# W2 moved into the B stage as eight 64x64 events, with weight rows on two DMA queues

## The chip, the cores and the metric

The kernel runs on one core of one Trainium2 chip. The metric is the device time of one execution in microseconds. All runs quoted are of the state called fast unless the text says otherwise. Engines: PE is TensorE, PEld its weight loads, DVE is VectorE, ACT is ScalarE, POOL is GpSimd, SP is SyncE, which here only issues DMAs.

## The reference, cut to what matters

Two attention blocks read the same `x` (2048 x 1024) and a gate mixes their outputs. Both have 32 heads of 32.

```python
# A: linear attention
q, k, v = split(x @ A_wqkv)
pq, pk = phi(q), phi(k)                    # phi(t) = (t+1 if t > 0 else exp(t)) + 1e-6
kv  = einsum("bhsd,bhse->bhde", pk, v)     # one 32x32 matrix per head
o   = einsum(pq, kv) / (einsum(pq, z) + 1e-6)
a   = o @ A_wo
# B: sliding window of 8 keys, dilation 2, softmax; b = (...) @ B_wo
return g * a + (1 - g) * b
```

Since `o @ A_wo` is linear in `kv`, the kernel folds the 32 small `kv` matrices into `A_wo` once. `z` is the sum of `pk` over `s`. The folded matrix is called W2, and it overwrites the tile `WoA`. Nothing reads W2 before the output stage, the last one.

## The kernel before: the parts that matter

The stages follow each other on TensorE: keys of A (`pk_ps`), G = xᵀ·phi(k) (`g_ps`), the small `kv` matrices (`kv_ps`), values of B mixed with the W2 events (the V stage), values of B and queries of A in turn (the query stage), the B stage (keys, queries, scores, outputs of the window attention, in 64x64 mode), and the output stage.

The first loads. TensorE needs `x` transposed and the key weights in order of `kt`, the 128-row slice of the contraction:

```python
load_wk(nc.scalar, 0)          # weight row kt on ScalarE's queue
load_xT(0, 1, 0, 4)            # a DMA transpose, on SyncE's queue
load_wk(nc.sync, 1)
load_xT(1, 1, 0, 4)
for kt in range(2, KT):        # KT = 8
    load_wk(nc.sync, kt)
    if kt % 2 == 0:
        load_xT(kt, 2, 0, 4)
```

W2 in the V stage, as four events of sixteen matmuls, each on its own 32x32 part of the array:

```python
def w2_event(g, half):
    w2p = [ps_1.tile([P, 512], F32, ...) for _ in range(4)]        # four PSUM tiles
    for j in range(4):
        for r in range(4):
            rs = slice(32 * r, 32 * r + 32)
            nc.tensor.matmul(w2p[r][32 * j:32 * j + 32, :],
                             lhsT=KVT[rs, 4 * g + j, (r % 2) * 32:(r % 2) * 32 + 32],
                             rhs=WoA[half][rs, 4 * g + j, :], start=True, stop=True)
    for r in range(4):
        (nc.scalar.copy if r % 2 else nc.vector.tensor_copy)(out=WoA[half][:, 4 * g + r, :], in_=w2p[r][:])
```

The B stage works in units: one unit is four 64x64 matmuls that run side by side. There are 64 units to a head block and eight head blocks. Other work is hung in between at a unit number. The score batches share one PSUM buffer (`ps_s`, one buffer of two banks):

```python
p_ = 64 * c + (43, 55, 75, 86, 97)[m // 4]           # cut: the last block differs a little
events.append((p_, lambda g=g: scores(g)))            # takes the tile with tag "s" of ps_s
events.append((p_ + 14, lambda g=g: pv(g)))
```

At the end of the query stage VectorE still has the last block of A's queries to finish (phi, then `normalize`: two passes of 1024 elements, some small ones, and the product with the reciprocal). That work needs the last matmuls of the query stage.

The softmax here doesn't subtract the row's maximum and nothing guards it: scores larger than these inputs give would overflow.

Of the kernel before, what the change touches and what calls it, by code (L numbers as in the profile page):

```python
# [9 lines left out]
ALU = mybir.AluOpType  # L10
BF16 = mybir.dt.bfloat16
F32 = mybir.dt.float32
# [3 lines left out]
P = 128  # L16
# [23 lines left out]
def kernel(  # L40
# [11 lines left out]
    nc = tc.nc  # L52
# [3 lines left out]
    x = A_x[0].rearrange("(m two) d -> two m d", two=2)  # L56
# [5 lines left out]
    H = 32  # L62
    Dh = D // H
    KT = D // P
# [29 lines left out]
    def load_xT(kt, n, t0, t1):  # L94
        nc.sync.dma_start_transpose(out=xT[:, kt:kt + n, t0 * P:t1 * P],  # L95
                                    in_=rows(x, t0 * P, t1 * P)[:, kt * P:(kt + n) * P])

    def load_wk(eng, kt):
        eng.dma_start(out=WkA[:, kt, :], in_=A_wqkv[kt * P:(kt + 1) * P, D:2 * D])  # L99

    ones = nc.const_aps.tensor(1.0, [P, P], BF16)
    with tc.manual_schedule(engines={SP, mybir.EngineType.Activation}):
        load_wk(nc.scalar, 0)
        load_xT(0, 1, 0, 4)
        load_wk(nc.sync, 1)
        load_xT(1, 1, 0, 4)
        for kt in range(2, KT):
            load_wk(nc.sync, kt)
            if kt % 2 == 0:
                load_xT(kt, 2, 0, 4)  # L110
        for t in range(4, NB):
            nc.sync.dma_start_transpose(out=xT[:, :, t * P:(t + 1) * P], in_=rows(x, t * P, (t + 1) * P))  # L112
        for t in range(0, NB, 4):
            load_rows(nc.sync, t, t + 4)
        gw_row = consts.tile([P, D], BF16, name="gw_row")
        nc.sync.dma_start(out=gw_row[:], in_=gate_w.partition_broadcast(P))  # L116
        WvA = load_w("WvA", A_wqkv, 2 * D, "wb")
        WoA = load_w("WoA", A_wo, 0, "wo")
        WvB = load_w("WvB", B_wqkv, 2 * D, "wc")
# [18 lines left out]
    for slot in range(2):  # L138
        nc.gpsimd.memset(qsel[:, slot:slot + 1], 0.0)
        for pair in range(2):  # L140
            r = 64 * pair + 32 * slot
# [3 lines left out]
    omg = consts.tile([P, NB], F32, name="omg")  # L145
    zrow = consts.tile([P, D], F32, name="zrow")
    KVT = consts.tile([P, KT, 64], BF16, name="KVT")

    small3 = ctx.enter_context(tc.tile_pool(name="small3", bufs=2))

    def phi(work, dst, pj):
        e = work.tile([P, 512], F32, name="e", tag="e")
# [4 lines left out]
    with tc.manual_schedule(engines={PE}):  # L157

        with ExitStack() as s1:
# [39 lines left out]


            side = []
            for t in range(1, NB):
                side.append(lambda t=t: nc.vector.tensor_tensor(
                    out=zacc[:], in0=zacc[:] if t > 1 else pk[:, 0, :], in1=pk[:, t, :], op=ALU.add))
            side.append(lambda: nc.gpsimd.partition_all_reduce(zrow[:], zacc[:], P, bass_isa.ReduceOp.add))
            for t in range(NB):
                side.append(lambda t=t: nc.vector.tensor_tensor_reduce(
# [24 lines left out]
            for g in range(2):  # L232
                kvp = ps_pj.tile([P, 512], F32, name="kv_ps", tag="pj")[:, 0:256].rearrange("p (c d) -> p c d", c=4)
                for c in range(4):
                    for kt in range(KT):
                        for j in range(2):
                            cols = slice(c * P + 64 * j, c * P + 64 * j + 64)
                            nc.tensor.matmul(kvp[64 * j:64 * j + 64, c, :], lhsT=WvA[g][:, kt, cols],
                                             rhs=G[g][:, kt, cols], start=(kt == 0), stop=(kt == KT - 1))
                nc.vector.tensor_copy(out=KVT[:, 4 * g:4 * g + 4, :], in_=kvp)  # L240
            WkB = load_w("WkB", B_wqkv, D, "wb")


# [28 lines left out]



            def w2_event(g, half):
                def go():
                    w2p = [ps_1.tile([P, 512], F32, name="w2_ps", tag="p1") for _ in range(4)]
                    for j in range(4):
                        for r in range(4):
                            rs = slice(32 * r, 32 * r + 32)  # L280
                            nc.tensor.matmul(w2p[r][32 * j:32 * j + 32, :],
                                             lhsT=KVT[rs, 4 * g + j, (r % 2) * 32:(r % 2) * 32 + 32],
                                             rhs=WoA[half][rs, 4 * g + j, :], start=True, stop=True)
                    for r in range(4):
                        (nc.scalar.copy if r % 2 else nc.vector.tensor_copy)(
                            out=WoA[half][:, 4 * g + r, :], in_=w2p[r][:])
                return go

            def v_units(t):
                def mm(half, kt, st):  # L290
                    if kt == 0:
                        st["pj"] = bank1()
                    nc.tensor.matmul(st["pj"][:], lhsT=xT[:, kt, t * P:(t + 1) * P], rhs=WvB[half][:, kt, :],  # L293
                                     start=(kt == 0), stop=(kt == KT - 1))
                    if kt < KT - 1:
                        return
                    v = Vst[t % 2]
                    nc.scalar.copy(out=v[:, half * 16:(half + 1) * 16, 0:Dh],  # L298
                                   in_=st["pj"][:].rearrange("p (h e) -> p h e", h=16))
                    if half == 1:  # L300
                        nc.sync.dma_start(out=vd[t * P:(t + 1) * P, :], in_=v.rearrange("p h e -> p (h e)"))
                        if t % 8 == 7:
                            load_v(t // 8)
                for half in range(2):
                    st = {}
                    for kt in range(KT):
                        yield lambda half=half, kt=kt, st=st: mm(half, kt, st)

            def normalize(t, pq, pn, prod):
                nc.vector.tensor_tensor(out=prod, in0=pq, in1=zrow[:], op=ALU.mult)  # L310
                den = small3.tile([P, H], F32, name="den", tag="den")
                nc.vector.tensor_reduce(out=den[:], in_=prod.rearrange("p (h e) -> p h e", h=H),
                                        axis=mybir.AxisListType.X, op=ALU.add)
                nc.vector.tensor_scalar(out=den[:], in0=den[:], scalar1=1e-6, scalar2=None, op0=ALU.add)
                nc.vector.reciprocal(out=den[:], in_=den[:])

                nc.vector.tensor_scalar(out=den[:], in0=den[:], scalar1=ratio[:, t:t + 1], scalar2=None, op0=ALU.mult)
                for g in range(2):
                    nc.vector.tensor_tensor(
                        out=pn[:, 512 * g:512 * g + 512].rearrange("p (r j e) -> p j r e", r=4, j=4),  # L320
                        in0=pq[:, 512 * g:512 * g + 512].rearrange("p (j r e) -> p j r e", r=4, j=4),
                        in1=den[:, 16 * g:16 * g + 16].rearrange("p (j r o) -> p j r o", r=4, o=1)
                        .broadcast_to([P, 4, 4, Dh]), op=ALU.mult)

            def qa_units(t, bank, evacuate):
                def mm(half, kt, st):
                    if kt == 0:
                        st["pj"] = bank()
                    nc.tensor.matmul(st["pj"][:], lhsT=xT[:, kt, t * P:(t + 1) * P], rhs=WqA[:, kt, half * 512:half * 512 + 512],  # L329
                                     start=(kt == 0), stop=(kt == KT - 1))  # L330
                    if kt == KT - 1:
                        evacuate(t, half, st["pj"])
                for half in range(2):
                    st = {}
                    for kt in range(KT):
                        yield lambda half=half, kt=kt, st=st: mm(half, kt, st)
# [5 lines left out]
                    normalize(t, pq, pn, prods[t % 2])  # L342
                    nc.sync.dma_start(out=pqd[t * P:(t + 1) * P, :], in_=pn)

            units = [u for t in range(4) for u in v_units(t)]
            w2_event(0, 0)()
            interleave(units, [(20, w2_event(0, 1)), (32, w2_event(1, 0)), (44, w2_event(1, 1))])
            for t in range(12):
                for u in v_units(4 + t):
                    u()  # L350
# [9 lines left out]
        with ExitStack() as s2:  # L360
# [139 lines left out]
            for g, (c, m, n) in enumerate(BATCHES):  # L500
                p_ = 64 * c + ((43, 55, 75, 86, 97) if c < KT - 1 else (43, 55, 75, 83, 92))[m // 4]
                events.append((p_, lambda g=g: scores(g)))
                events.append((p_ + (14 if c < KT - 1 or m < 8 else 12), lambda g=g: pv(g)))

            def between(a, b):
                return [(p_ - a, f) for p_, f in events if a <= p_ < b]

# [31 lines left out]
            def qa_output(t, half):  # L539
                def lhsT(r, kt, j):  # L540
                    return xT[64 * r:64 * r + 64, kt, t * P + 64 * j:t * P + 64 * j + 64]

                def rhs(r, kt):
                    return WqA[64 * r:64 * r + 64, kt, half * 512:half * 512 + 512]

                def evacuate(ps, part):
                    if part == 0:
                        nc.scalar.copy(out=raw[:, t - 12, half * 512:(half + 1) * 512], in_=ps[:])
                return lhsT, rhs, evacuate
# [93 lines left out]
```

## Time and profile before

| | before |
|---|---|
| median of 5 runs | 474.04 us |
| profiled span | 472.34 us |
| TensorE busy | 466.3 us (99%) |
| start to first `g_ps` matmul | 61.44 us |
| last `kv_ps` to first query matmul (V stage and W2) | 19.18 us |
| query stage | 79.52 us |
| B start to first scores | 9.62 us |

TensorE is busy nearly all the time, so a change counts only where TensorE issues less or waits less. The busy table of the page of before gives engine, busy us, share, instructions:

```profile
PE 466.3 (99%) x5735; PEld 244.8 (52%) x5765; DVE 277.3 (59%) x601; ACT 169.1 (36%) x272; POOL 15.3 (3%) x30
```

The timeline of TensorE around one W2 event of before: start, length, engine, line, operation, out<-in, shape, count.

```profile
122.55 1.24 PE L293 MATMUL p_ps<-WvB,xT 128*128 128x512 bf16 x5
123.72 0.43 PE L281 MATMUL w_ps<-WoA,KVT 32*32 32x512 bf16 x16
124.09 2.76 PE L293 MATMUL p_ps<-WvB,xT 128*128 128x512 bf16 x12
126.78 0.43 PE L281 MATMUL w_ps<-WoA,KVT 32*32 32x512 bf16 x16
```

The lengths overlap (a 128x512 matmul is 0.38 us long, 0.216 us after the one before), so one reads starts. The last V matmul before the event starts at 123.41 us, the first after it at 124.09, where 0.216 us is the rule between 128x512 matmuls. The event costs 0.47 us.

The timeline of TensorE at the start, of before; brackets give idle time and what ended it:

```profile
4.74 4.14 PE L167 MATMUL pk_ps<-WkA,xT 128*128 128x512 bf16 x15
9.19 0.39 PE L167 MATMUL pk_ps<-WkA,xT 128*128 128x512 bf16 x1 [0.31 <-DMA xT<-in_A_x_dram]
9.86 2.32 PE L167 MATMUL pk_ps<-WkA,xT 128*128 128x512 bf16 x10 [0.28 <-DMA WkA<-in_A_wqkv_dram]
```

Two waits: the third transpose and weight row 3. From start to start they cost 0.47 and 0.45 us.

VectorE's timeline at the B start (217.51 us) of before:

```profile
218.25 0.43 DVE L154 TENSOR_SCALAR e<-e 128x512 f32<-128x512 f32 x1
218.71 0.69 DVE L155 SCALAR_TENSOR_TENSOR tmp<-p_ps,e 128x512 bf16<-128x512 f32 x1
219.43 1.22 DVE L310 TENSOR_TENSOR tmp<-tmp,zrow 128x1024 f32<-128x1024 bf16 x1
220.69 1.22 DVE L312 TENSOR_REDUCE den<-tmp 128x32 f32<-128x1024 f32 x1
...
222.55 0.24 DVE L317 TENSOR_SCALAR den<-den,ratio 128x32 f32<-128x32 f32 x1
222.83 1.29 DVE L319 TENSOR_TENSOR tmp<-tmp,den 128x512 bf16<-128x512 bf16 x2
```

There is no hole in it: for 6.6 us of the B stage VectorE has nothing to spare.

### The profile page before, as it was taken

Reading aid. Unit: us, or ns where it says so; the run is one execution under the profiler, and the core shown is the slowest. Engines: PE = TensorE matmul, PEld = TensorE weight load, DVE = VectorE, ACT = ScalarE, POOL = GpSimd, SP = SyncE. Lnnn points to the kernel's source line nnn. Section 1 sums busy time; section 2 is a strip of 40 time slices with the busy share of each in tenths; the row PEclk is TensorE's granted clock in tenths of the full one; section 3 lists DMA queues with packets and bytes.
Section 4 is the critical chain, followed back from the end, with each engine's and each line's share of the span. In section 5 each row is a group of like instructions: output and inputs, shape, how many; then the busy total and the mean of one; then the engine's idle time right before and its main releaser. Section 6 shows DMA issues by size and latency. Waiting matters only on the chain.

```text
span 472.3 us, 13141 instructions
## 1 busy us (share of the span) xinstructions
PE 466.3 (99%) x5735; PEld 244.8 (52%) x5765; DVE 277.3 (59%) x601; ACT 169.1 (36%) x272; POOL 15.3 (3%) x30
## 2 busy tenths in 40 slices
PE   8999999999999999999999999999999999999997
PEld 5444444444444444445666666666664444444444
DVE  0496689990329999999567676767560049800000
ACT  1343321102533333333555555555551134221122
POOL 3300000500000000000000000000000000000000
PEclk9999999999999999999999999999999999999999
DMA  9999970000644233527326526432463843221101
GB/s 199 196 240 377 348 266 0 0 1 0 207 135 108 98 138 132 154 97 243 108 57 104 105 55 95 101 82 63 93 164 67 187 113 78 70 54 45 35 33 46
DMA packets 96716, 55.40 MB, mean 117 GB/s; under 512 B 70162, under 2 KB 86546, under 8 KB 96658
## 3 DMA queue, kind: packets, MB, share of 16 engines
q1 hardware_dynamic: 91618, 50.10, 41.4%
q10 hardware_dynamic: 5040, 4.46, 3.0%
q8 instruction: 45, 0.74, 0.7%
q14 instruction: 13, 0.11, 0.1%
HBM read 26.10 MB, written 15.86 MB: 89 GB/s over the span
## 4 chain that ended last, share of the span: by engine, by line
PE 86%; SPq 11%; DMA 2%; issue 1%; ACT 0%
PE q_ps L387 27%; PE d_ps L584 12%; PE p_ps L293 12%; PE e_ps L584 11%; PE g_ps L218 11%; PE p_ps L329 9%; SPq L112 4%; SPq L82 4%; DMA WvB<-in_B_wqkv_dram 2%; PE po L466 2%; PE s2b L444 2%; SPq L95 1%; SPq L99 1%; SPq L116 1%; SPq L90 0%
## 5 line engine op out<-in xcount | busy, mean ns | idle before, releaser
L387 PE MATMUL q_ps<-xT,WqB 64*64 64x512 bf16 x1024 | 68.3, 377 | 0.0
L387 PE MATMUL q_ps<-xT,WkB 64*64 64x512 bf16 x1024 | 67.9, 377 | 0.0
L154 DVE TENSOR_SCALAR e<-e 128x512 f32<-128x512 f32 x64 | 27.0, 422 | 64.5 <-ACT e L153 64.5
L293 PE MATMUL p_ps<-WvB,xT 128*128 128x512 bf16 x249 | 57.0, 379 | 0.4 <-issue 0.2
L167 PE MATMUL pk_ps<-WkA,xT 128*128 128x512 bf16 x251 | 56.0, 381 | 0.9 <-DMA xT<-in_A_x_dram 0.3
L218 PE MATMUL g_ps<-pk,xrow 128*128 128x512 bf16 x251 | 55.2, 379 | 0.3
L449 ACT ACTIVATE PT<-s2b 128x928 bf16<-128x928 f32 (+4 forms) x40 | 34.2, 854 | 45.5 <-PE s2b L444 45.5
L451 DVE TENSOR_TENSOR PT<-PT,mask 128x928 bf16<-128x928 bf16 (+4 forms) x40 | 23.6, 590 | 38.1 <-ACT PT L449 38.1
L329 PE MATMUL p_ps<-WqA,xT 128*128 128x512 bf16 x189 | 43.2, 379 | 0.2
L584 PEld LDWEIGHTS <-pqT 128*128 128x128 bf16 x272 | 26.0, 98 | 29.8 <-issue 0.4
L167 PEld LDWEIGHTS <-xT 128*128 128x128 bf16 x256 | 25.1, 99 | 31.4 <-issue 1.3
L584 PEld LDWEIGHTS <-OBT 128*128 128x128 bf16 x272 | 26.0, 98 | 29.3
L218 PEld LDWEIGHTS <-xrow 128*128 128x128 bf16 x256 | 25.0, 98 | 30.2
L293 PEld LDWEIGHTS <-xT 128*128 128x128 bf16 x256 | 24.7, 98 | 30.2 <-issue 0.9
L387 PEld LDWEIGHTS <-WkB 64*64 64x64 bf16 x1024 | 31.6, 107 | 15.4 <-issue 0.4
L387 PEld LDWEIGHTS <-WqB 64*64 64x64 bf16 x1024 | 31.3, 106 | 15.4 <-issue 0.7
L153 ACT ACTIVATE e<-pk_ps 128x512 f32<-128x512 f32 x32 | 18.9, 597 | 41.3 <-PE pk_ps L167 37.0
L298 ACT CAST tmp<-p_ps 128x512 bf16<-128x512 f32 x32 | 18.8, 589 | 35.5 <-PE p_ps L293 29.0
L584 PE MATMUL d_ps<-WoA,pqT 128*128 128x512 bf16 (+1 forms) x133 | 30.7, 369 | 0.2
L584 PE MATMUL d_ps<-WoB,OBT 128*128 128x512 bf16 (+1 forms) x134 | 30.7, 369 | 0.1
L329 PEld LDWEIGHTS <-xT 128*128 128x128 bf16 x192 | 18.8, 98 | 22.6
L584 PE MATMUL e_ps<-WoB,OBT 128*128 128x512 bf16 (+2 forms) x133 | 29.7, 363 | 0.2
(61 smaller groups left out, 484.4 us busy)
## 6 DMA issues: line engine op xcount, KB each, us to landing
vd<-tmp SPq DMA_DIRECT2D x16, 264.0 KB
xrow<-in_A_x_dram SPq DMA_DIRECT2D x4, 1024.0 KB
out_dram<-osb ACTq DMA_DIRECT2D x31, 128.0 KB
pqd<-tmp SPq DMA_DIRECT2D x12, 256.0 KB
WvA<-in_A_wqkv_dram SPq DMA_DIRECT2D x2, 1024.0 KB
WoA<-in_A_wo_dram SPq DMA_DIRECT2D x2, 1024.0 KB
WvB<-in_B_wqkv_dram SPq DMA_DIRECT2D x2, 1024.0 KB
WqA<-in_A_wqkv_dram SPq DMA_DIRECT2D x1, 2048.0 KB
```

Of the source, the lines that this page charges most:

```text
L82: nc.sync.dma_start(out=w[:], in_=src[:, c0:c0 + 512].rearrange("(kt p) n -> p kt n", p=P))
L112: nc.sync.dma_start_transpose(out=xT[:, :, t * P:(t + 1) * P], in_=rows(x, t * P, (t + 1) * P))
L153: nc.scalar.activation(out=e[:], in_=pj[:], func=ACT.Exp)
L154: nc.vector.tensor_scalar(out=e[:], in0=e[:], scalar1=1.0, scalar2=1e-6, op0=ALU.min, op1=ALU.add)
L167: nc.tensor.matmul(pj[:], lhsT=xT[:, kt, t * P:(t + 1) * P], rhs=WkA[:, kt, half * 512:half * 512 + 512], start=(kt == 0), stop=(kt == KT ...
L218: nc.tensor.matmul(pj[:], lhsT=xrow[:, t, kt * P:(kt + 1) * P], rhs=pk[:, t, half * 512:(half + 1) * 512], start=(t == 0), stop=(t == NB - 1))
L293: nc.tensor.matmul(st["pj"][:], lhsT=xT[:, kt, t * P:(t + 1) * P], rhs=WvB[half][:, kt, :], start=(kt == 0), stop=(kt == KT - 1))
L329: nc.tensor.matmul(st["pj"][:], lhsT=xT[:, kt, t * P:(t + 1) * P], rhs=WqA[:, kt, half * 512:half * 512 + 512], start=(kt == 0), stop=(kt ...
L387: nc.tensor.matmul(banks[o][64 * j:64 * j + 64, :], lhsT=lhsT(r, kt, j), rhs=rhs(r, kt), start=first and kt == 0, stop=kt == KT - 1, skip_ ...
L449: nc.scalar.activation(out=pt[:, :, 0:W_], in_=s2b[:].rearrange("p a b s -> p (a b) s")[:, :, 0:W_], func=ACT.Exp, scale=SCALE)
L451: nc.vector.tensor_tensor(out=pt[:, :, 0:W_], in0=pt[:, :, 0:W_], in1=mask[:, None, base:base + W_].broadcast_to([P, 4, W_]), op=ALU.mult)
L584: nc.tensor.matmul(st["ps"][:, 0:n], lhsT=lhsT, rhs=W[c0 // 512][:, c, c0 % 512:c0 % 512 + n], start=(side == 0 and c == 0), stop=(side == ...
```

## The change

Intent: spare TensorE the mode changes of the W2 events by putting W2 into the stage that is in 64x64 mode anyway, and get the first weights sooner by issuing them on two queues. To fit 64x64, two 32x32 head matrices are laid into one 64x64 block-diagonal matrix (the rest is zero). The rows of W2 come out in another order. A's query columns follow it, by a strided operand. The core of the diff (cut: the z sums in the new order, the `KVT` fill and copies, the simpler product in `normalize`, the same strided operand for the late queries):

```diff
-        for kt in range(2, KT):
-            load_wk(nc.sync, kt)
-            if kt % 2 == 0:
-                load_xT(kt, 2, 0, 4)
+        for kt in (2, 4, 6):
+            src = ones if kt == 2 else WkA[:, kt - 4 if kt == 4 else 2, :]
+            nc.scalar.copy(out=WkA[:, kt, 0:1], in_=src[:, 0:1])
+            load_wk(nc.scalar, kt)
+            load_xT(kt, 2, 0, 4)
+            load_wk(nc.sync, kt + 1)
...
+    def by_row_half(ap, r):
+        return ap.rearrange("p (q c r x) -> p r c q x", q=2, c=4, r=2)[:, r]
...
-                    nc.tensor.matmul(... rhs=WqA[:, kt, half * 512:half * 512 + 512],
+                    nc.tensor.matmul(... rhs=by_row_half(WqA[:, kt, :], half),
...
-            units = [u for t in range(4) for u in v_units(t)]
-            w2_event(0, 0)()
-            interleave(units, [(20, w2_event(0, 1)), (32, w2_event(1, 0)), (44, w2_event(1, 1))])
+            for t in range(4):
+                for u in v_units(t):
+                    u()
...
+            def w2(c, half):
+                ps = ps_s.tile([P, 2, 512], F32, name="w2_ps", tag="s")
+                for r in range(2):
+                    for q in range(2):
+                        nc.tensor.matmul(ps[64 * q:64 * q + 64, r, :], lhsT=KVT[64 * r:64 * r + 64, c + 4 * q, :],
+                                         rhs=WoA[half][64 * r:64 * r + 64, c + 4 * q, :], start=True, stop=True)
+                for r in range(2):
+                    (nc.scalar.copy if r else nc.vector.tensor_copy)(out=WoA[half][:, c + 4 * r, :], in_=ps[:, r, :])
+
+            for i in range(8):
+                events.append((9 + 4 * i, lambda i=i: w2(i % 4, i // 4)))
```

The one-column `nc.scalar.copy` is a gate: ScalarE cannot issue row 4 before row 0 has landed, nor row 6 before row 2.

More of the change, by code (lines that the diff above doesn't have):

```diff
@@ L147 @@
     KVT = consts.tile([P, KT, 64], BF16, name="KVT")
+    nc.gpsimd.memset(KVT[:], 0.0)
     small3 = ctx.enter_context(tc.tile_pool(name="small3", bufs=2))
+    def by_row_half(ap, r):
+        return ap.rearrange("p (q c r x) -> p r c q x", q=2, c=4, r=2)[:, r]
     def phi(work, dst, pj):
@@ L201, with add_z @@
             side = []
+            def add_z(t):
+                for r in range(2):
+                    z = zacc[:, 512 * r:512 * r + 512].rearrange("p (c q x) -> p c q x", c=4, q=2)
+                    nc.vector.tensor_tensor(out=z, in0=z if t > 1 else by_row_half(pk[:, 0, :], r),
+                                            in1=by_row_half(pk[:, t, :], r), op=ALU.add)
             for t in range(1, NB):
-                side.append(lambda t=t: nc.vector.tensor_tensor(
-                    out=zacc[:], in0=zacc[:] if t > 1 else pk[:, 0, :], in1=pk[:, t, :], op=ALU.add))
+                side.append(lambda t=t: add_z(t))
             side.append(lambda: nc.gpsimd.partition_all_reduce(zrow[:], zacc[:], P, bass_isa.ReduceOp.add))
@@ L239 @@
                                              rhs=G[g][:, kt, cols], start=(kt == 0), stop=(kt == KT - 1))
-                nc.vector.tensor_copy(out=KVT[:, 4 * g:4 * g + 4, :], in_=kvp)
+                for r in range(4):
+                    d = slice((r % 2) * 32, (r % 2) * 32 + 32)
+                    nc.vector.tensor_copy(out=KVT[32 * r:32 * r + 32, 4 * g:4 * g + 4, d], in_=kvp[32 * r:32 * r + 32, :, d])
             WkB = load_w("WkB", B_wqkv, D, "wb")
@@ L271, in bank1 @@
                 return ps_pj.tile([P, 512], F32, name="p1_ps", tag="pj")
-            def w2_event(g, half):
-                def go():
-                    w2p = [ps_1.tile([P, 512], F32, name="w2_ps", tag="p1") for _ in range(4)]
-                    for j in range(4):
-                        for r in range(4):
-                            rs = slice(32 * r, 32 * r + 32)
-                            nc.tensor.matmul(w2p[r][32 * j:32 * j + 32, :],
-                                             lhsT=KVT[rs, 4 * g + j, (r % 2) * 32:(r % 2) * 32 + 32],
-                                             rhs=WoA[half][rs, 4 * g + j, :], start=True, stop=True)
-                    for r in range(4):
-                        (nc.scalar.copy if r % 2 else nc.vector.tensor_copy)(
-                            out=WoA[half][:, 4 * g + r, :], in_=w2p[r][:])
-                return go
             def v_units(t):
@@ L317, in normalize @@
                 nc.vector.tensor_scalar(out=den[:], in0=den[:], scalar1=ratio[:, t:t + 1], scalar2=None, op0=ALU.mult)
-                for g in range(2):
-                    nc.vector.tensor_tensor(
-                        out=pn[:, 512 * g:512 * g + 512].rearrange("p (r j e) -> p j r e", r=4, j=4),
-                        in0=pq[:, 512 * g:512 * g + 512].rearrange("p (j r e) -> p j r e", r=4, j=4),
-                        in1=den[:, 16 * g:16 * g + 16].rearrange("p (j r o) -> p j r o", r=4, o=1)
-                        .broadcast_to([P, 4, 4, Dh]), op=ALU.mult)
+                nc.vector.tensor_tensor(out=pn.rearrange("p (h e) -> p h e", h=H), in0=pq.rearrange("p (h e) -> p h e", h=H),
+                                        in1=den[:, :, None].broadcast_to([P, H, Dh]), op=ALU.mult)
             def qa_units(t, bank, evacuate):
@@ L328, in mm @@
                         st["pj"] = bank()
-                    nc.tensor.matmul(st["pj"][:], lhsT=xT[:, kt, t * P:(t + 1) * P], rhs=WqA[:, kt, half * 512:half * 512 + 512],
+                    nc.tensor.matmul(st["pj"][:], lhsT=xT[:, kt, t * P:(t + 1) * P], rhs=by_row_half(WqA[:, kt, :], half),
                                      start=(kt == 0), stop=(kt == KT - 1))
@@ L503 @@
                 events.append((p_ + (14 if c < KT - 1 or m < 8 else 12), lambda g=g: pv(g)))
+            def w2(c, half):
[4 more added lines that the diff above has]
+                                         rhs=WoA[half][64 * r:64 * r + 64, c + 4 * q, :], start=True, stop=True)
+                for r in range(2):
+                    (nc.scalar.copy if r else nc.vector.tensor_copy)(out=WoA[half][:, c + 4 * r, :], in_=ps[:, r, :])
+            for i in range(8):
+                events.append((9 + 4 * i, lambda i=i: w2(i % 4, i // 4)))
             def between(a, b):
@@ L543, in rhs @@
                 def rhs(r, kt):
-                    return WqA[64 * r:64 * r + 64, kt, half * 512:half * 512 + 512]
+                    return by_row_half(WqA[64 * r:64 * r + 64, kt, :], half)
                 def evacuate(ps, part):
```

## The prediction

> **What bounds the kernel.** TensorE: 466.3 of 472.3 us busy (busy table), granted clock 1.00. 128x512 matmuls follow each other at 0.216 us (timeline), so time counts only where TensorE issues or waits less.
>
> **Removed: W2 in the V stage.** Four events of sixteen 32x32 matmuls sit among 128x128 matmuls. The timeline shows 123.41 -> 124.09 between two V matmuls where 0.216 is the rule: 0.47 us per event (0.37 for the first), of which only 0.216 is streaming. The rest is the mode change: the Trainium skill, "TensorEngine Tiling (Array Packing)", Key Properties, says that changing mode drains TensorE, and the trace agrees (0.31 us before the event, 0.32 after). All critical: **-1.8 us**.
>
> **Two queues for the key weights.** At the start TensorE waits twice (timeline): 0.47 us for transposed x (9.19), 0.45 us for weight row 3 (9.86); then no more. SyncE issues 1.2 to 1.5 us per transpose, 0.5 per weight row; with rows moved to ScalarE those two issues come 0.6 and 1.3 us earlier. But the DMA engines are shared and nearly full from 5 us. **-0.6 us** (0.2 to 0.9).
>
> **Added: eight W2 events in the B stage.** Four 64x64 matmuls at once stream in 0.216 us without a mode change: **+1.7 us**. Block-diagonal weights need twice the streaming of the sixteen-tile form, so the saved drain is spent again.
>
> **The new wait.** W2's buffer is the one score buffer, so each event waits for both copies of the previous one, and TensorE keeps its order. Row half 0 is copied by VectorE, also in order, and VectorE is late when B starts (217.51): the last block's exp comes at 217.62, its phi and normalization run without a hole to 224.12, +6.6 us (timeline); the fused multiply saves perhaps 0.06. Event 0 issues at +1.9, its VectorE copy (0.69) ends about +7.3, event 1 wants to start at +3.0: **+4.3 us** of standing TensorE. Later events want 1.08 us spacing; matmul, copy and semaphore take about 1.13. The sixth waits for a ScalarE copy behind two key evictions (1.07): +0.5. The eighth waits behind the query evictions: +1.0. With the rest, **+6.0 us**. An old 0.1 us wait at 226.49 vanishes. The idle hole may also lower the clock (same skill, "TensorE: Matmul & The Clock Gate", Part 1: after a free-running idle window of about 3.4 us); first real matmuls here ran at 0.427 us, so a relapse costs one to two us: weighed, +0.3.
>
> **Off the path, zero:** z sums split in two (15 x about 0.1 us; VectorE idles 10.5 us before the KV copy), eight small KV copies, strided query weights (64-element runs: I expect 0.216 us as before).
>
> **Sum:** 473.9 - 1.8 - 0.6 + 1.7 + 6.0 - 0.1 + 0.3 = about 479.4 us; as VectorE's copy might be scheduled earlier (then 474 to 475), I say **478.5 us, range 474.0 to 481.5**. Faster by over 2%: 0.01; within 2%: 0.95; slower by over 2%: 0.04.
>
> **What would show it.** V stage (118.9 to 138.0) shorter by 1.8 us; query matmuls still 0.216; first g matmul 0.6 us before 63.1; in B one TensorE hole of about 4 us, three us in, ended by VectorE's W2 copy, and short ones at the sixth and eighth event; first scores about 7.6 us later after B's start than before; later key blocks unchanged at 15.86 us; output stage unchanged.
>
> **What would make it wrong.** VectorE's copy not behind the normalization; the strided operand slowing matmuls (10% of the query stage's would be 4 us); the clock falling after the hole; the second queue delaying transposes.

## The result, and the profile after

The changed kernel took 485.68 us (median of 5, 484.82 to 486.04), against 474.04 (473.84 to 476.67) in the same rounds. The ratio is 1.0228, with a 95% interval of 1.0202 to 1.0254: slower by over 2%.

The spans of the two profiles, cut at the same matmuls:

| stretch | before | after | difference |
|---|---|---|---|
| start to first `g_ps` matmul | 61.44 | 63.74 | +2.30 |
| to last `kv_ps` matmul | 57.37 | 57.37 | 0.00 |
| to first query matmul (V stage) | 19.18 | 17.40 | -1.78 |
| query stage, to B start | 79.52 | 79.52 | 0.00 |
| B start to first scores | 9.62 | 20.60 | +10.98 |
| first scores to first output matmul | 131.55 | 131.55 | 0.00 |
| output stage to the end | 113.65 | 113.76 | +0.11 |
| span | 472.34 | 483.95 | +11.61 |

Two places lose. All else is as intended, and the strided operand is free: the query stage is 79.52 us in both.

**The start.** The timeline of TensorE at the start, after:

```profile
4.66 1.89 PE L175 MATMUL pk_ps<-WkA,xT 128*128 128x512 bf16 x8
8.41 1.90 PE L175 MATMUL pk_ps<-WkA,xT 128*128 128x512 bf16 x8 [1.87 <-DMA xT<-in_A_x_dram]
11.53 0.39 PE L175 MATMUL pk_ps<-WkA,xT 128*128 128x512 bf16 x1 [1.22 <-DMA xT<-in_A_x_dram]
12.16 2.10 PE L175 MATMUL pk_ps<-WkA,xT 128*128 128x512 bf16 x9 [0.24 <-DMA WkA<-in_A_wqkv_dram]
```

The second transpose, in time before, is now waited for, the third longer than before. The busy times by stretch of the changed kernel (stretch, length, busy of PE, PEld, DVE, ACT, POOL, granted clock, DMA share, GB/s):

```profile
5.00:7.00 2.00, 1.55 (x8) 0.49 (x5) 0.00 (x0) 0.00 (x0) 0.00 (x0) 1.00 1.15 237
7.00:9.00 2.00, 0.58 (x3) 0.31 (x4) 0.00 (x0) 0.19 (x1) 0.00 (x0) 1.00 1.11 170
9.00:11.00 2.00, 1.32 (x7) 0.39 (x4) 0.00 (x0) 0.00 (x0) 0.63 (x2) 1.00 1.09 136
```

The last column matters: from 7 to 11 us the DMA engines move 170 and 136 GB/s. The same stretches of before have 218 and 302:

```profile
7.00:9.00 2.00, 1.82 (x8) 0.68 (x7) 0.00 (x0) 0.00 (x0) 0.08 (x1) 1.00 1.25 218
9.00:11.00 2.00, 1.53 (x7) 0.66 (x8) 0.00 (x0) 0.00 (x0) 2.00 (x5) 1.00 1.20 302
```

The engines are nearly as busy (share 1.11 and 1.09, before 1.25 and 1.20) but deliver less.

**The B stage.** The timeline of the changed kernel from the first W2 event to the fourth, with the other lines left out:

```profile
220.00 0.60 PE L507 MATMUL w_ps<-WoA,KVT 64*64 64x512 bf16 x4
...
223.23 0.68 DVE L510 CAST WoA<-w_ps 128x512 bf16<-128x512 f32 x1
223.83 1.22 DVE L320 TENSOR_TENSOR tmp<-tmp,den 128x1024 bf16<-128x1024 bf16 x1
223.95 0.58 ACT L510 CAST WoA<-w_ps 128x512 bf16<-128x512 f32 x1 [3.56 <-DVE WoA L510]
224.59 0.41 PE L507 MATMUL w_ps<-WoA,KVT 64*64 64x512 bf16 x4 [3.12 <-ACT WoA L510]
...
225.04 0.69 DVE L510 CAST WoA<-w_ps 128x512 bf16<-128x512 f32 x1
...
225.77 0.58 ACT L510 CAST WoA<-w_ps 128x512 bf16<-128x512 f32 x1 [1.23 <-DVE WoA L510]
...
226.40 0.64 PE L507 MATMUL w_ps<-WoA,KVT 64*64 64x512 bf16 x4 [0.55 <-ACT WoA L510]
```

Three things are to be seen. TensorE stands 3.12 us before the second event. ScalarE's copy never starts before VectorE's has ended. From the second event to the third 1.82 us pass (224.59 to 226.40), where 1.08 us of work is in between. The waits of the changed kernel between 218 and 239 us (who, for whom: us in total, times, longest):

```profile
ACT WoA L510 <- DVE WoA L510: 11.1, 8, 3.6
...
PE w_ps L507 <- ACT WoA L510: 6.2, 6, 3.1
```

All eight ScalarE copies waited for VectorE's. Last, the clock of the changed kernel, in the column before DMA share:

```profile
224.50:226.40 1.90, 1.27 (x20) 0.68 (x20) 1.24 (x2) 0.67 (x3) 0.00 (x0) 1.00 0.21 80
226.40:230.10 3.70, 3.70 (x40) 2.04 (x40) 1.38 (x2) 0.91 (x4) 0.00 (x0) 0.54 0.51 160
```

About 1.8 us after the hole the clock fell to about half for 3.7 us, and groups of four matmuls followed each other at up to 0.427 us. Nine groups from 226.40 to 230.02 took 3.62 us instead of 1.94.

The 10.98 us in the B stage, from start to start of matmuls less the 0.216 us of a group: streaming of W2 1.73 (8 x 0.216), first hole 3.28, slow clock 1.68, waits at the other events and at the first scores 0.70 + 0.32 + 0.70 + 0.70 + 1.48 + 0.27 = 4.17. The sum is 10.86; 0.12 is small change.

### The profile page after: what moved, and what is told of

Read it like the earlier page. It is cut to its first block, busy times and chain, and to the rows that moved or that the text cites. A ratio compares the mean times of both kernels' runs of the same rounds, so it can differ in the third digit from the quotient of the medians.

```text
span 484.0 us, 13117 instructions
## 1 busy us (share of the span) xinstructions
PE 470.4 (97%) x5733; PEld 245.9 (51%) x5733; DVE 277.2 (57%) x606; ACT 169.9 (35%) x275; POOL 15.8 (3%) x31
## 4 chain that ended last, share of the span: by engine, by line
PE 93%; DVE 2%; DMA 1%; ACT 1%; SPq 1%; issue 0%; DVEq 0%
PE q_ps L385 24%; PE d_ps L594 12%; PE p_ps L295 11%; PE g_ps L232 11%; PE e_ps L594 11%; PE pk_ps L175 11%; PE p_ps L327 9%; PE po L464 2%; PE s2b L442 2%; DMA WkA<-in_A_wqkv_dram 1%; DVE WoA L510 1%; SPq L95 1%; ACT WoA L510 1%; PE w_ps L507 0%; PE kv_ps L252 0%; DVE tmp L312 0%
## 5 line engine op out<-in xcount | busy, mean ns | idle before, releaser
L385 PE MATMUL q_ps<-xT,WkB 64*64 64x512 bf16 x1024 | 69.7, 383 | 0.0
L594 PE MATMUL e_ps<-WoA,pqT 128*128 128x512 bf16 (+2 forms) x136 | 30.0, 363 | 0.0
```

Of the source, the lines that this page charges most:

```text
L385: nc.tensor.matmul(banks[o][64 * j:64 * j + 64, :], lhsT=lhsT(r, kt, j), rhs=rhs(r, kt), start=first and kt == 0, stop=kt == KT - 1, skip_ ...
L594: nc.tensor.matmul(st["ps"][:, 0:n], lhsT=lhsT, rhs=W[c0 // 512][:, c, c0 % 512:c0 % 512 + n], start=(side == 0 and c == 0), stop=(side == ...
```

## The experiments

The theory. At the start, rows on the second queue take the DMA engines from transposes that are needed sooner. In the B stage, three things add up on the one W2 buffer: VectorE is late, the two copies of an event run one after the other, and the hole lowers the clock. Rivals: the gates on ScalarE, the order of the loads, or differences between chips for the start; copies or block-diagonal matmuls that cost wherever they stand for the B stage. Sixteen runs, all with the right result.

### Which part loses what: x1_old_loads and x2_loads_only

x1 is the changed kernel with the old load loop put back (the first hunk of the diff reversed). x2 is the kernel before with only that hunk.

> The changed kernel with the key-weight loads put back as they were before. Theory (the second queue costs at the start, the W2 events cost in the B stage, the two add up): first g matmul back at about 61.4 us (63.7 in the changed kernel), B start to first scores still about 20.6 us, time 483.4 us. Rival (the later start is something else in the change, such as the KV memset or other scheduling): first g stays near 63.7 and the time near 485.7.

> The kernel before with only the key-weight loads of the change. Theory: first g matmul at about 63.7 us instead of 61.4, everything after shifted by as much, time 476.3 us. My prediction on record would have it at 473.3.

Measured: x1 484.24 us (ratio 1.021, 1.0176 to 1.0244), first `g_ps` at 61.30 us, B start to first scores 20.59. x2 475.83 us (ratio 1.0022, 0.9993 to 1.0051), first `g_ps` at 63.04. The profiles separate the parts cleanly: the loads make the late start, the W2 events make the B stage. The times agree less well: x2 is 1.2 us over the median of before (474.62), whose runs went from 473.86 to 476.56, so this interval alone shows no loss. The loss in the start is read from the profiles and settled by x13 to x15.

### VectorE's lateness: x5_copies_act

On x1, both copies on ScalarE:

```diff
-                    (nc.scalar.copy if r else nc.vector.tensor_copy)(out=WoA[half][:, c + 4 * r, :], in_=ps[:, r, :])
+                    nc.scalar.copy(out=WoA[half][:, c + 4 * r, :], in_=ps[:, r, :])
```

> x1 with both W2 copies on ScalarE, none on VectorE. Theory (the first hole is VectorE still busy with the last normalization, and the hole causes the slow clock): no hole over 1.5 us, no matmuls at half rate, but two ScalarE copies in a row still make each event wait about 0.5 us and the key and query evictions more, B start to first scores about 16.5 us instead of 20.6, time about 479.3 us. Rival (VectorE's lateness matters little, the single buffer and the copies in a row are all): 18.5 to 20.6 us to first scores and 481.5 us or more.

Measured: 478.89 us (ratio 1.009), B start to first scores 15.74 us. No wait over 1.1 us from start to start, no slow matmul: the clock over the whole stretch of x5 is 1.00.

```profile
215.40:231.00 15.60, 12.52 (x205) 6.64 (x205) 8.00 (x13) 11.64 (x25) 0.00 (x0) 1.00 0.45 157
```

So the first hole is VectorE's, and the slow clock goes with it. The events still follow at 1.58 us where nothing else disturbs: two ScalarE copies in a row.

### The copies one after the other: x6_two_tiles

On x1, the second half of each event goes to a bank of the output accumulator, a PSUM tile of its own, whose fill with ones moves behind the last event (cut: that move, and the operands that follow):

```diff
-                ps = ps_s.tile([P, 2, 512], F32, name="w2_ps", tag="s")
+                ps = [ps_s.tile([P, 2, 512], F32, name="w2_ps", tag="s")[:, 0, :], po[:, 1, :]]
```

> x1 with the two halves of a W2 event in two PSUM tiles (row half 1 in the output accumulator, whose fill with ones moves behind the events). Theory (ScalarE's copy stands behind VectorE's copy only because both read one PSUM tile): ScalarE's copies start with VectorE's, the time from event to event in undisturbed places falls from 1.82 to about 1.15 us, the first hole by 0.6, B start to first scores about 17 us, time about 480 us (478.5 if the clock then does not fall). Rival (the order of the copies has another reason): 1.82 us from event to event and 483.4 us as in x1.

Measured: 480.69 us (ratio 1.0132), B start to first scores 17.86 us; hoped for were 17. The timeline of x6 at the second event:

```profile
221.38 0.68 DVE L507 CAST WoA<-w_ps 128x512 bf16<-128x512 f32 x1
222.11 0.40 PE L504 MATMUL w_ps<-WoA,KVT 64*64 64x512 bf16 x2 [2.50 <-DVE WoA L507]
222.12 0.40 PE L504 MATMUL po<-WoA,KVT 64*64 64x512 bf16 x2
222.62 0.59 ACT L507 CAST WoA<-po 128x512 bf16<-128x512 f32 x1 [3.21 <-PE po L504]
223.11 0.69 DVE L507 CAST WoA<-w_ps 128x512 bf16<-128x512 f32 x1
```

ScalarE's copy no longer waits for VectorE's; here it even runs first. The order of the copies came from the shared PSUM tile: both copies still write `WoA`, as before. The halves of an event lie in two banks (512 f32 each), and the Trainium skill, "PSUM — Partial Sum Buffer", Specifications (TRN2), says that ScalarE and VectorE read PSUM in parallel at full bandwidth as long as there is no bank collision. x6 agrees in that two copies from different tiles overlap with lengths unchanged (0.69 and 0.59). So it was the program's ordering by tile, not the copies' speed. The best spacing was 1.22 us, the others more, from VectorE's other work and the slow clock. TensorE stood only 2.50 us here, and the clock fell all the same. In time it does not follow the hole by a fixed step: in x6 and the changed kernel it fell 1.7 and 1.8 us after work had resumed, in x1 it was down when the second event started, after 3.3 us without a matmul. Nor does 2.50 us seem to be enough each time: of the four runs of x6 two have a mean clock of 0.995 and 0.996, two of 0.999.

### The clock by itself: x8_filled_hole

On x1, 14 groups of useless matmuls in front of the second event, into the output accumulator before its fill (cut: the function `fill`, and the fill with ones, which moves as in x6):

```diff
+            events.append((13, lambda: fill(14)))
```

> x1 with 56 useless 64x64 matmuls (14 groups, 3.0 us, into the output accumulator before its fill with ones) in front of the second W2 event, so that TensorE works while it would have stood. Theory (the eight groups of matmuls at 0.427 us after the hole are the clock falling because TensorE stood idle over 3 us): all matmuls stay at 0.216 us, granted clock 1.00, first scores about 1.7 us earlier than in x1, time about 481.7 us. Rival (the slow matmuls have another cause, such as operands or copies): still there, 483.4 us.

Measured: 483.76 us (ratio 1.0202), no slow matmul, and B start to first scores 20.06 us, only 0.53 less than x1. The stretch of x8 that held the slow matmuls in the changed kernel:

```profile
224.50:236.10 11.60, 7.98 (x132) 4.25 (x130) 6.03 (x9) 5.76 (x11) 0.00 (x0) 1.00 0.26 90
```

The idle hole causes the slow clock; this much of the theory holds (all nine runs of the changed kernel and x1 have a mean clock of 0.993 to 0.996, the four of x8 1.000). Its worth does not. With the clock at 1.00 every event waits for the copies again, 1.82 us from one to the next; at half clock TensorE took so long that the copies were done. Two delays hid each other, and of 1.7 us only 0.5 is to be had.

### W2 where the buffer is free: x7_spread

On x1, one event in each head block, behind the second score batch:

```diff
-                events.append((9 + 4 * i, lambda i=i: w2(i % 4, i // 4)))
+                events.append((64 * i + 65, lambda i=i: w2(i % 4, i // 4)))
```

> x1 with the same eight W2 events, one in each of the eight head blocks, put behind the second score batch where the score buffer has over 2 us before its next use. Theory (all the loss over the 1.7 us of streaming is waiting for the one buffer at the start of B): no TensorE wait at any W2 event, B stage longer than before by 1.7 us only, V stage shorter by 1.8, so the time is 474.2 us, the same as before. Rival (the added copies on VectorE and ScalarE or the block-diagonal matmuls cost wherever they stand): over 476 us.

Measured: 476.93 us (ratio 1.0048, 1.0021 to 1.0076), 2.7 us worse than expected. The waits at W2 are gone and B start to first scores is 9.63 us. But first scores to last scores is 127.11 us against 123.26 before: +3.85 instead of +1.73. The third score batch of each block comes 5.50 us after the second, 5.03 before: it finds the buffer not yet copied out, since the copies stand behind the query evictions. The other 0.6 us is at the very end, where the span of this run ends 3.52 us after the last matmul instead of 2.89; that time varied from 2.89 to 3.70 us among the fast profiles. It seems to go with the edit: in x7 ScalarE's queue took 0.97 us to issue the last store but one, 0.34 in before, and five of the seven profiles with W2 in the B stage show such an issue there (0.71 to 1.14 us), but none of the ten fast ones with W2 in the V stage. Why is open.

### Both repairs: x11_spread_shifted

On x7, the third score batch two units later (in the last head block the fourth one unit later as well), and weight row 1 moved as in x4 below.

> x7 with two edits: the third score batch of each head block two units later (so that the W2 copies end before it), and weight row 1 straight on the second queue as in x4. Theory: the 0.25 us that each W2 event still cost in x7 vanishes, B stage longer than before by 1.7 us only, first g at about 61.0 us, time 473.5 to 474.5 us, so at best the time of before: the W2 move saves 1.8 us and costs 1.7. Rival (the added copies cost elsewhere too): over 475.5 us.

Measured: 474.49 us against 474.00 (ratio 1.0006, 0.999 to 1.0023). No TensorE wait at any W2 event, and first to last scores 124.98 us, +1.72: the streaming alone. The V stage is shorter by 1.77. The shift cost 0.50 us after the last scores. This answers what the move of W2 is worth when nothing waits: nothing. It saves 1.77 and streams 1.72. That x11 comes out level with before in the sum is not the move's doing alone: the profile has the earlier start of x4 (first `g_ps` 0.45 us sooner), which pays for half of what the shift (0.50) and a late end as in x7 (0.38) cost.

### The start: x3_gate_later, x9_gate_again, x10_ungated, x12_one_queue_order, x4_row1_second

All are the kernel before with other load orders. x3 is x2 with each row on the second queue gated on the row before it:

```diff
-            src = ones if kt == 2 else WkA[:, kt - 4 if kt == 4 else 2, :]
+            src = WkA[:, kt - 2, :]
```

> x2 (before plus new loads) with one edit: each row on the second queue waits for the previous row of that queue, so row 2 is issued at about 4.3 us instead of 2.3. Theory (rows of the second queue take the DMA engines' time from the transposes of x that TensorE needs first): the wait for the second transpose of x, 2.0 us in the changed kernel, falls under 0.5 us, and first g comes at 61.4 to 62.5 us, time 474 to 475. Rival (the rows gated on ScalarE simply come too late): later gates make it worse, first g after 63.7 us, time over 476.3.

Its profile (823 us, clock 0.558) says nothing of the start. The fast runs took 474.73 to 475.51 us, before 474.03 (ratio 1.0015, 0.9986 to 1.0044): inconclusive. The same kernel again:

> The kernel of x3 again, whose profile fell in a slow state, to see its start: before plus the new loads, row 2 issued only when row 0 has landed. Theory (row 2 on the second queue takes the DMA engines from the second transpose of x): the wait for that transpose is under 0.5 us (2.0 to 2.2 in the changed kernel and x2), first g at 61.5 to 62.5 us; what is left comes at the third transpose. Rival (gates on ScalarE make rows late): the waits are for weight rows, not for x, and first g is over 63 us.

Measured: 473.73 us (ratio 0.9994), first `g_ps` at 61.61, no wait for the second transpose. That looked like the theory, but the next run did not. x10 has no gates at all (the `nc.scalar.copy` deleted):

> x2 with the gates taken out: rows 0, 2, 4 and 6 are issued on the second queue one after the other at the start. Theory (rows ahead of their turn push back the transposes that are needed sooner): the wait for the second transpose of x grows from 2.2 to about 4 us, later waits shrink, first g after 63.5 us, time 476.5 us or more. Rival (the gates are the cost): waits shrink, first g before 62 us, time under 475.

Measured: 473.87 us (ratio 0.9997), first `g_ps` at 61.36. The theory fell here: rows ahead of their turn did no harm. (Rows 2 and 4 were issued at 1.25 and 1.74 us; row 6 in fact only at 7.41.) The wait for the second transpose was 0.9 us, not 4.

x12 has the order of the change on SyncE's queue alone:

> Before with the order of the change but on one queue: on SyncE each pair of transposes is issued ahead of its two weight rows, none of the rows after row 0 on ScalarE. Theory (the second queue is the cost, not the order): first g within 0.5 us of before (61.0 to 61.9), time 473.6 to 474.5, no wait for x over 1 us. Rival (the order is the cost): first g over 62.5 us, time over 475.

Measured: 474.26 us (ratio 1.0004), first `g_ps` at 61.59, but with a wait of 1.2 us for the second transpose. In the sum the order alone costs nothing.

x4 moves one row only:

```diff
         load_xT(0, 1, 0, 4)
-        load_wk(nc.sync, 1)
+        load_wk(nc.scalar, 1)
```

> Before with one edit: weight row 1 is issued by ScalarE straight after row 0, so that SyncE comes to every later issue about 0.56 us sooner; no row is in the second queue while later transposes run. Theory: the early DMA engines have time to spare, so transposes land sooner, the 0.9 us of waits at 9 to 10 us shrink to about 0.4, first g at 60.9 us, time 473.5 us. Rival (any row on the second queue delays the transposes): first g at 61.5 or later, time 474.2 or more.

Measured: 473.81 us (ratio 0.9987, 0.9967 to 1.0008), first `g_ps` at 61.04. The first matmul came a microsecond later, at 5.77, and nothing waited after it. Right in the sum, not in the way.

### Which row: x13_loads_again, x14_row4_later, x15_row2_later, x16_gate_third

After x10 the question was whether the loss was the chip's (x2, x9 and x10 had run on two chips) or one row's. These four ran on one chip. x13 is x2. x14 lets row 2 go at once but gates row 4 on row 2 (x13: on row 0), and row 6 on row 4 (x13: on row 2). x15 holds rows 2 and 4 until row 0 has landed. x16 is x3.

> The kernel of x2 (before plus the new loads) again, on the chip of the three that follow. If the new loads cost and not the chip of x2: first g at 63.0 to 63.8 us, two waits for x of over 0.7 us, time 1.3 to 2.3 us over before. If it was the chip: first g under 62 us and time within 0.5 us of before.

> x2 with row 2 still issued at once on the second queue but row 4 only when row 2 has landed (and row 6 when row 4 has). Theory A (row 2 ahead of the second transpose of x is the cost): the wait for that transpose stays at about 2 us, first g 62.5 us or later. Theory B (row 4, which runs beside the transposes and row 3 that are needed first, is the cost): the second and third transposes and row 3 come in time or nearly, first g at 61.4 to 62.2, time within 0.7 us of before.

> x2 with rows 2 and 4 both issued when row 0 has landed (row 6 when row 2 has). Theory A (row 2 early is the cost): the second transpose of x comes in time, first g at 61.4 to 62.2. Theory B (row 4 beside the third transpose and row 3 is the cost): the wait for the third transpose and row 3 stays at 1 us or more, first g at 62.5 us or later.

> The kernel of x3 and x9 a third time (row 2 when row 0 has landed, row 4 when row 2 has, row 6 when row 4 has): it was 1.2 us over before on one chip and 0.3 under it on another. Both theories: no wait over 0.7 us, first g at 61.4 to 61.9, time within 0.5 us of before. If it is over before by 1 us here, the start depends on the chip or the moment more than on the gates, and a difference of 1 us in a start is not to be read from one run.

| | rows 2 / 4 issued, us | first `g_ps`, us | median, us | ratio (95%) |
|---|---|---|---|---|
| x13 | 2.32 / 4.14 | 63.13 | 475.93 | 1.0022 (0.9998 to 1.0046) |
| x14 | 2.31 / 7.47 | 61.19 | 473.72 | 0.9982 (0.9962 to 1.0002) |
| x15 | 3.98 / 6.00 | 62.49 | 475.13 | 1.0016 (0.9994 to 1.0038) |
| x16 | 3.93 / 8.21 | 61.80 | 474.60 | 1.0014 (0.9981 to 1.0048) |

x13 and x14 differ in two gates, those of row 4 and row 6. All six runs of x13 (474.50 to 477.00 us) are slower than all six of x14 (473.46 to 474.36). x13 at the start, TensorE's timeline:

```profile
4.16 1.89 PE L169 MATMUL pk_ps<-WkA,xT 128*128 128x512 bf16 x8
7.91 1.90 PE L169 MATMUL pk_ps<-WkA,xT 128*128 128x512 bf16 x8 [1.86 <-DMA xT<-in_A_x_dram]
10.91 0.39 PE L169 MATMUL pk_ps<-WkA,xT 128*128 128x512 bf16 x1 [1.10 <-DMA xT<-in_A_x_dram]
```

x14, the same view:

```profile
4.74 9.56 PE L169 MATMUL pk_ps<-WkA,xT 128*128 128x512 bf16 x38
```

The one wait left, 0.25 us at 7.65 us, is too short to split the line. The wait of x13 for the second transpose is not the loss: x14 used that transpose at 7.65 us, x13 at 7.91, only 0.26 us later. x13 waited longer because TensorE started sooner (4.16 us against 4.74) and at once at 0.216 us per matmul, where x14's first five starts lie 0.427 us apart. The loss is at the third transpose, used at 9.39 us in x14 and at 10.91 in x13, and at row 3 (0.43 us from start to start in x13, none in x14). The rates by stretch, first of x13, then of x14:

```profile
7.00:9.00 2.00, 1.09 (x6) 0.51 (x6) 0.00 (x0) 0.19 (x1) 0.00 (x0) 1.00 1.12 161
9.00:11.00 2.00, 0.90 (x5) 0.29 (x4) 0.00 (x0) 0.00 (x0) 1.12 (x4) 1.00 1.04 190
...
7.00:9.00 2.00, 1.91 (x10) 0.71 (x9) 0.00 (x0) 0.19 (x1) 0.00 (x0) 1.00 1.20 296
9.00:11.00 2.00, 2.00 (x11) 0.94 (x10) 0.00 (x0) 0.00 (x0) 1.24 (x4) 1.00 1.13 360
```

With row 4 issued 3.3 us later the DMA engines move 296 and 360 GB/s between 7 and 11 us; in x13 it was 161 and 190. So it is the kernel and not the chip. The starts of the DMA packets in the traces tell which row. In x13 the packets of row 4 began between 6.79 and 9.91 us, among those of the third transpose (6.61 to 10.15), which landed at 10.86. In x14 they began between 9.50 and 10.38, after the third transpose's (6.81 to 7.95), which landed at 8.54. Row 6's packets began at 12.45 us or later in both, after the waits, so its gate is not the cause. The row is row 4, which the gate on row 0 lets go so that it runs beside the third transpose and row 3, both needed sooner. This also fits x10, where row 4's packets began between 4.22 and 6.23 us and the third transpose's only at 6.99, and x15, where row 4's (9.01 to 10.26) ran beside row 3's (8.27 to 10.18) and TensorE stood 1.36 us for row 3. Row 2 early (x14) is harmless, row 2 late does not help (x15). x16 had waits of about 1.2 us at the start and one run of 478.50 us (mean clock 0.996, the other five 0.999 or more), so half a microsecond of a start is not to be read from one run.

Why the engines deliver so much less in that mixture, rather than merely share, stays open. In x13 the 2 KiB packets of the second queue (row 4's) that began between 7 and 8 us took 283 ns in the mean, and 88 ns between 12 and 13 us. But x10 had the second queue beside transposes too, earlier, at 307 GB/s from 3 to 5 us. Mixing as such is not shown to be slow.

No version beats before beyond the noise: the best is x14, 0.18% faster with an interval that ends at 1.0002.

## Why the prediction was wrong

It said 478.5 us (474.0 to 481.5). The measured 485.68 lies outside. Point by point:

- **Removed, -1.8 us: right.** The V stage is 1.78 us shorter.
- **Added streaming, +1.7 us: right.** x11 shows 1.72 with no waits.
- **"Two queues for the key weights ... -0.6 us": wrong in sign.** It measured +2.3 in the profiled run, 1.6 and 1.7 in x2 and x13 by first `g_ps` against the 61.44 of before. I counted the issue time that SyncE saves and named the shared engines as a mere damper. The step that failed is the assumption that a row sent early only uses spare time. Row 4 ran beside the third transpose and row 3, which are needed sooner, and the rate fell: the third transpose landed at 10.86 us instead of 8.54 (x13 against x14). The Trainium skill, "DMA: Bandwidth & Descriptors", "Issuing engines are not separate DMA queues", says that such DMAs run on the same 16 engines and interleave, and that a second issuer saves issue time only. The trace agrees, in that row 4's packets start among the third transpose's, and goes further: the total rate between 7 and 11 us was 161 and 190 GB/s, against 296 and 360 in x14.
- **"Event 0 ... event 1 wants to start at +3.0: +4.3 us": the mechanism right, the size off.** The hole was 3.28 us. VectorE did not keep the order that I assumed: the program had put the first W2 copy before the last product (223.23 and 223.83 us in the trace). ScalarE's copy behind it gave back part of that.
- **"Later events want 1.08 us spacing; matmul, copy and semaphore take about 1.13": this is the other step that failed.** I let the two copies of an event run side by side, as in the V stage of before (119.45 and 119.49 us in the trace). They ran one after the other, and the spacing was 1.82 us. Waits at the later events and the first scores were 4.17 us instead of about 1.7. x6 shows that the shared tile orders them.
- **"a relapse costs one to two us: weighed, +0.3": it came in full.** Nine groups took 1.68 us too long. Of that, 0.53 was real loss (x8).
- **Strided operand, z sums, KV copies, zero: right.** Query stage 79.52 us in both, and 57.37 us from first `g_ps` to the last KV matmul in both.

One number of the prediction was read wrongly. "First g matmul 0.6 us before 63.1" took 63.1 from the chain of waits of before:

```profile
52.08 11.08 DMA WvB<-in_B_wqkv_dram
63.16 0.01 issue
63.17 10.74 PE g_ps L218 x49
```

The chain steps over to a DMA at 63.17 us; the first `g_ps` matmul in the timeline starts at 61.44. A chain tells where one path runs, not where a stage begins.

## What to carry to other kernels

Before moving work into a stage because its mode fits, ask what empties its buffer: here 0.9 us of mode changes were saved (the 1.78 us of the V stage less 4 x 0.216 of streaming), as much was spent on zeros in the block-diagonal matmuls, and 7.5 us of waiting for a single buffer and 1.7 us of slow clock came on top. Two engines that read one PSUM tile may be put in order by the program even where their banks differ, so look for an engine waiting for its partner in the waits before counting their copies as parallel. A load issued early on a second queue may cost (row 4 in x13) or not (x10): see beside what its packets run, gate it behind what is needed sooner, and check the rate that the DMA engines deliver, not their busy share.

## What the Trainium skill lacked or had wrong

- "TensorE: Matmul & The Clock Gate", Part 1, puts the fall of the clock after an idle window of about 3.4 us. Here TensorE stood 3.12 us (changed kernel) and 2.50 us (x6), and the clock fell 1.7 to 1.8 us after work had resumed, to 0.54 over 3.7 us in the changed kernel; in x1 it was down when work resumed. The same part does say that frequent short stops can make the clock go up and down, but not how long they have to be. Waits of up to 1.3 us (x8) did not lower it.
- "DMA: Bandwidth & Descriptors" says that queues interleave on the same engines. It does not say that a weight row beside DMA transposes can lower the total rate: 161 and 190 GB/s with row 4 early (x13), 296 and 360 with it late (x14), between 7 and 11 us. Why is not shown, and x10, with row 4 out of the way, had 291 and 363.
- "TensorEngine Tiling (Array Packing)" says that a mode change drains TensorE but gives no size. Here an event of 32x32 matmuls with 0.216 us of streaming cost 0.47 us among 128x128 matmuls, so some 0.25 us for the two changes of mode.
- No page has that matrices of 32x32 laid block-diagonally into 64x64 tiles need twice the streaming: 8 x 0.216 us here against 4 x 0.216.
